# Attention scores in 64-key tiles: five full units for two head groups, an output product in two phases, tokens ahead of weights

## The chip, the core and the metric

The kernel runs on one core of a Trainium2 chip. The metric is the device time of one execution in microseconds; lower is better. On the core, PE (TensorE) multiplies matrices into PSUM, eight banks of 512 fp32 columns on 128 partitions; ACT (ScalarE) evaluates exponentials and GELU; DVE (VectorE) and POOL (GpSimd) do elementwise work; SP issues most DMAs.

## What is computed

Two equal layers over 2048 tokens of width 576. Each is a residual attention block and a residual MLP block:

```python
x = x + _A_ref(_layernorm(x), A_wqkv, A_wo)      # 32 heads of 18, causal, window 256
x = x + _B_ref(_layernorm(x), B_w1, B_b1, B_w2, B_b2)   # 576 -> 4608 -> 576, tanh GELU

scores = jnp.einsum("bhqd,bhkd->bhqk", q, k) * (Dh ** -0.5)
mask = (idx[:, None] - idx[None, :] >= 0) & (idx[:, None] - idx[None, :] < W)   # W = 256
p = _softmax(jnp.where(mask, scores, -1e9))
o = jnp.einsum("bhqk,bhkd->bhqd", p, v)
```

A query sees itself and the 255 tokens before it. Data are bf16; the residual is kept in fp32.

## The kernel before

The work is cut into eight chunks (`CH`, k = 0 to 7): layer 0 has chunks 0 to 3, layer 1 chunks 4 to 7, each of four token tiles of 128. In a chunk, `qkv` projects the normalized tokens, `E` does attention for eight head groups g of four heads j, `tail` multiplies by `wo` and adds the residual, `G_part` does the first MLP product with GELU in three parts, `mm2` the second. Attention of chunk k is interleaved with the MLP of chunk k-1.

Each head's 18 values are padded to 32, so the four heads of a group stand on four 32-row strips of `qT` and `kT`, and four matmuls work side by side in the array. Scores are computed transposed, keys on partitions and queries in columns. `units_of` lists which 128-key tiles meet which queries. A 128-key tile needs three query tiles (its own, partly masked, the next, and the one after, partly masked), so the six key tiles that touch a chunk take 1 + 2 + 3 + 3 + 2 + 1 = 12 blocks of 128 columns, in three units of 512 columns for each group. Chunks 0 and 4 have no earlier keys and take 9 blocks, in units of 384, 512 and 256 columns.

`scores` (L777) issues a unit: its matmuls (L789) go to two pairs of PSUM banks, one bank for a head; two exponentials on ACT (L798), each over two heads, write `pT`; POOL zeroes the masked triangles by `affine_select` (L819). `pT` has PS = 6 slots. `pv` (L824) multiplies all units of a group by the values: 24 matmuls (L834) over 128 key rows, each 20 columns wide (18 values and a column of ones for the softmax's denominator), the four heads on four 32-column strips, into one bank of 7, 6, 5, 4 (`OUT`, shared with `FILL`, the banks of `qkv`, `tail` and `mm2`). DVE transposes the result (L845), takes the reciprocal of the denominator and scales (L851).

The matmuls of `qkv` and `tail` share L699; `G_part` starts each six blocks with six 64-row matmuls (L919) and goes on with 128-row ones (L931); `mm2` is L960.

What decides the order is a planner, `Plan.schedule`. Every operation is a task with an estimated cost, a priority and data dependences; the planner places the task that can start first on its engine, and the order so made is written out with semaphores. `PL.nudge` holds a table of offsets to the priorities by stage, `SWITCH` is the cost charged for a change of PE's tiling (`mode`), and `fifo` keeps tasks of one kind in the order of their listing. Within PE no semaphore is waited for, since matmuls there are in order.

At the start, SP loads the tokens of chunk 0 into `w2_sb` (as `x_in`), ACT issues the six loads of `wqkv` and then loads its table; DVE clears the four output banks (L601), and then layer norm of the four tiles (L620, L643), a transpose on PE (L657) and the projections follow.

Of the kernel before, what the change touches and what calls it, by code (L numbers as in the profile page):

```python
# [40 lines left out]
class Sched:  # L41
# [23 lines left out]
    def add(self, eng, fn, reads=(), writes=(), dma=None, ring=4):  # L65
# [11 lines left out]
        for w in writes:  # L77
            for rd in self.readers.get(w, ()):
                if rd[2] != eng or rd[3]:
                    want(rd[:3])  # L80
            lw = self.last_write.get(w)
            if lw is not None and not (eng == "pe" and lw[2] == "pe"):
                want(lw)
# [76 lines left out]
class Task:  # L160
    __slots__ = ("idx", "eng", "fn", "reads", "writes", "cost", "lat", "prio", "dma", "ring", "handles", "alloc", "move", "desc",
                 "npred", "succ", "ready", "end", "plain", "fifo", "hold", "stage", "mode")
# [24 lines left out]
class Plan:  # L187
# [18 lines left out]
    def add(self, eng, fn, reads=(), writes=(), dma=None, ring=4, cost=0.1, lat=0.1, prio=0.0, alloc=(), fifo=None, plain=False, after=(), move=0.0, desc=0, hold=False, mode="f"):  # L206
# [4 lines left out]
                 plain=plain, move=move, desc=desc, fifo=fifo, hold=hold, stage=stage, mode=mode)  # L211
# [31 lines left out]
    def keep_warm(self, a, b, bank_free, extra):  # L243
# [5 lines left out]
        if n < 1 or not banks:  # L249
# [4 lines left out]
                 dma=None, ring=4, alloc=(), handles=(), plain=False, move=0.0, desc=0, fifo=None, hold=False, stage="", mode="f")  # L254
        extra.append((a, t))

    def schedule(self):
# [56 lines left out]
        while len(order) < n:  # L314
# [80 lines left out]
            for s, data in t.succ:  # L395
                same = s.eng == t.eng == "pe"
                s.ready = max(s.ready, st + t.cost + (t.lat if data and not same else 0.0))
                s.npred -= 1
                if s.npred == 0:
                    released[s.eng].append(s)  # L400
# [3 lines left out]
        for st, t in order:  # L404
# [3 lines left out]
            else:  # L408
                self.S.add(t.eng, t.fn, names(t.reads), names(t.writes), dma=t.dma, ring=t.ring)
# [8 lines left out]
FEED_UNTIL = 40.0  # L418
# [3 lines left out]
def build_kernel(nc, A_x, A_wqkv, A_wo, B_x, B_w1, B_b1, B_w2, B_b2, out):  # L422
# [11 lines left out]
    CUTS = (0, 3, 6, 8)  # L434
# [6 lines left out]
    PS = 6  # L441
    PVG = [()] * 8
    PVLAG = 1
# [6 lines left out]
    NQN = 6  # L450
    WB = 6
    TOPF = D - 512

# [9 lines left out]
    PL.nudge = {"b": 29.4, "ea0": -2.66, "ld0": 0.01, "ld0+": -29.79, "eb0": 0.53, "ec0": 3.31, "le0+": 114.63, "q1.0": -118.82, "q1.1":  # L463
                -98.11, "q1.2": -0.91, "q1.3": -7.44, "t0": -5.22, "ea1": -89.48, "ga0": -171.5, "ga0+": 5.04, "eb1": -15.16, "ma0": 12.04,
                "ma0+": -17.91, "gb0": -145.98, "ec1": -2.99, "le1+": 16.44, "le1": -20.83, "mb0": -3.03, "q2.1": 45.54, "q2.2": 88.61,
                "q2.3": 55.86, "t1": -120.53, "gc0": -19.84, "gc0+": -25.1, "ln3": 57.08, "mc0": 4.28, "mc0+": 148.11, "ga1": -4.06, "ga1+":
                -6.33, "eb2": -3.01, "ma1": 5.64, "ma1+": 13.09, "gb1": -0.44, "ec2": 3.21, "mb1": 7.94, "mb1+": -24.34, "q3.0": 14.13,
                "q3.1": 131.09, "q3.2": 4.89, "q3.3": 1.84, "t2": -15.58, "gc1": 7.36, "gc1+": -31.57, "mc1": 17.31, "mc1+": -1.81, "ga2":
                -27.48, "ga2+": 158.23, "eb3": 36.01, "ma2": 50.85, "ma2+": 24.11, "gb2": 23.88, "gb2+": 71.77, "ec3": -0.31, "mb2": 60.21,
                "mb2+": -145.98, "q4.0": 0.58, "q4.1": 63.81, "q4.2": 55.53, "t3": 61.03, "gc2": 154.1, "gc2+": 8.93, "ln5": 14.44, "ea4":  # L470
                19.04, "mc2": 63.19, "ga3": 18.64, "ga3+": 0.44, "eb4": 14.59, "ma3": 30.2, "ma3+": 0.16, "gb3": -9.23, "gb3+": -6.16,
                "mb3": 45.14, "q5.0": 113.74, "q5.1": 29.89, "q5.2": -8.93, "q5.3": 76.56, "t4": -2.66, "gc3": 88.61, "gc3+": -48.97, "ln6":
                -15.57, "ea5": -72.82, "mc3": -2.47, "mc3+": 76.5, "ga4+": -33.16, "eb5": 2.91, "ma4": 29, "ma4+": 17.98, "gb4": -4.52,
                "gb4+": -7.43, "mb4": 59.81, "mb4+": -8.12, "q6.0": 1.38, "q6.1": 19.98, "q6.2": -18.44, "q6.3": 63.81, "gc4": 92.87,
                "gc4+": 84.52, "ln7": 31.11, "ea6": -2.66, "mc4": 24.73, "mc4+": 0.51, "ga5": 11.4, "ga5+": 1.49, "eb6": -0.34, "ma5":
                52.45, "ma5+": -6.49, "gb5": -32.33, "gb5+": 51.26, "ec6": -3.2, "mb5": 0.24, "mb5+": -3.62, "q7.0": 24.18, "q7.2": 137.8,
                "q7.3": 1.6, "t6": -24.34, "gc5": 5.59, "gc5+": -171.5, "ea7": 41.87, "mc5": 136.49, "mc5+": -1.6, "ga6": -32.64, "eb7":
                31.31, "ma6": 44.85, "ma6+": -1.66, "gb6": 0.02, "gb6+": -4.59, "ec7": -0.12, "mb6": 104.87, "mb6+": 63.38, "t7": -16.91,
                "gc6+": -0.75, "mc6": -119.39, "mc6+": -8.02, "ga7": -61.44, "ga7+": -11.43, "ma7": -14.13, "ma7+": 9.77, "gb7": 1, "mb7":
                3.96, "mb7+": -8.3, "gc7": 53.28, "mc7": 65.68, "": 0.88}  # L480
# [26 lines left out]
    rstd = sb("rstd", [P, NT], FP32)  # L507
    warm = sb("warm", [P, 256], BF16)
    ident = sb("ident", [P, P], BF16)
    b1in = sb("b1in", [NF, P], BF16)  # L510
# [43 lines left out]
    def dma(q, out_, in_, reads=(), writes=(), cls="w", ring=8, **kw):  # L554
# [4 lines left out]
        kw.setdefault("move", n / (330e3 if cls != "xr" else 165e3))  # L559
# [24 lines left out]

    w_load(0)
# [13 lines left out]
    for i in OUT:  # L599
        b = Bank((i,))  # L600
# [545 lines left out]
```

## Time and profile before

| | |
|---|---|
| median of 3 runs | 894.56 us (893.44 to 896.13) |
| profiled execution: its time | 897.23 us |
| its span, first to last instruction | 895.5 us |
| mean granted clock of PE | 0.998 |
| PE busy | 864.4 us (97%) |
| ACT busy | 615.8 us (69%) |
| DVE busy | 410.1 us (46%) |
| POOL busy | 366.2 us (41%) |

The busy time of PE is that of pipelined matmuls, whose recorded lengths overlap: a 288-column matmul is recorded with 286 ns, but the next starts 122.5 ns later. What a burst of matmuls costs is therefore read from its first start to the first start of the burst after it. Groups of instructions are named by the line that issued them, an engine and the tiles written and read; the time behind the last bar is how long the engine was idle before them, with the instruction that ended most of it.

### The profile page before, as it was taken

The page shows a single profiled execution, that of the slowest core. Times are in us where ns is not written, and L with a number is a line of the kernel's source. Part 1 is how long each engine was busy: PE and PEld are TensorE (multiplying, and loading weights), DVE is VectorE, ACT ScalarE, POOL GpSimd, SP SyncE. Part 2 cuts the span into 40 slices and gives each one's busy share as a digit, 9 for nine tenths or more (in the row PEclk, how much of TensorE's full clock was granted, in tenths as well). Part 3 has the DMA queues.
Part 4 walks back from the last instruction along what each step waited for, and adds up shares of the span by engine and source line. Part 5 has one row for each costly group of instructions (what it writes and reads, how often), then busy time and mean ns, then how long its engine had stood idle before and what let it go on. Part 6 is the DMA issues. An engine that isn't in the chain of part 4 may idle for free.

```text
span 895.5 us, 19577 instructions
## 1 busy us (share of the span) xinstructions
PE 864.4 (97%) x7849; PEld 506.5 (57%) x7901; DVE 410.1 (46%) x969; ACT 615.8 (69%) x737; POOL 366.2 (41%) x504
## 2 busy tenths in 40 slices
PE   5898999999999999999999999999999999999998
PEld 4555455656566565665655655556556545556665
DVE  6789223863357351763427633375134523161111
ACT  3976888577767788366773868747777689844443
POOL 3677544274244662224431544416444266231100
PEclk9999999999999999999999999999999999999999
DMA  6788537742477333853457342682537632446431
GB/s 177 139 172 173 179 119 182 178 109 81 149 166 158 120 120 98 183 124 121 130 119 181 71 158 86 143 198 67 165 119 147 184 125 71 144 126 176 153 96 50
DMA packets 182649, 122.25 MB, mean 137 GB/s; under 512 B 107424, under 2 KB 181024, under 8 KB 182560
## 3 DMA queue, kind: packets, MB, share of 16 engines
q1 hardware_dynamic: 179152, 115.47, 49.5%
q0 software_dynamic: 1584, 3.54, 1.5%
q10 hardware_dynamic: 1824, 1.99, 0.7%
q8 instruction: 63, 1.03, 0.5%
q14 instruction: 26, 0.21, 0.1%
HBM read 91.28 MB, written 2.36 MB: 105 GB/s over the span
## 4 chain that ended last, share of the span: by engine, by line
PE 54%; DVE 1%; issue 1%; DMA 1%; ACT 1%; POOL 0%
PE ps L960 21%; PE ps L931 18%; PE ps L699 6%; PE ps L789 3%; PE ps L919 3%; PE ps L834 3%; ACT pT L798 1%; DVE x_res L880 0%; DMA xnTa<-xn 0%; DVE st_all L620 0%; DMA xnTm<-xn 0%; DVE xn L643 0%; DVE xn L648 0%; POOL rstd L633 0%; DVE xn L883 0%
## 5 line engine op out<-in xcount | busy, mean ns | idle before, releaser
L819 POOL TENSOR_SCALAR_AFFINE_SELECT pT<-pT 128x512 bf16<-128x512 bf16 (+1 forms) x368 | 283.5, 794 | 266.6 <-ACT pT L798 262.0
L798 ACT ACTIVATE pT<-ps 128x1024 bf16<-128x1024 f32 (+2 forms) x384 | 345.8, 972 | 58.3 <-PE ps L789 57.8
L934 ACT ACTIVATE hT<-ps,b1col 128x512 bf16<-128x512 f32 x288 | 197.8, 687 | 192.8 <-PE ps L931 188.3
L960 PE MATMUL ps<-w_sb,hT 128*128 128x288 bf16 x2304 | 309.5, 287 | 0.2
L960 PEld LDWEIGHTS ps<-w_sb,hT 128*128 128x128 bf16 x2304 | 213.9, 98 | 81.9 <-issue 24.9
L931 PE MATMUL ps<-xnTm,w_sb 128*128 128x512 bf16 x1100 | 255.0, 380 | 4.9 <-issue 3.2
L931 PEld LDWEIGHTS ps<-xnTm,w_sb 128*128 128x128 bf16 x1152 | 109.6, 98 | 137.0 <-issue 19.1
L880 DVE TENSOR_TENSOR x_res<-ps,x_res 128x288 f32<-128x288 f32 x216 | 95.9, 448 | 169.0 <-PE ps L960 158.4
L699 PE MATMUL ps<-wqkv,xnTa 128*128 128x288 bf16 x960 | 136.0, 289 | 3.5 <-DVE qn L742 1.9
L845 DVE STREAM_TRANSPOSE oq<-ps 128x512 f32<-128x512 f32 x64 | 45.8, 715 | 179.0 <-PE ps L834 178.8
L699 PEld LDWEIGHTS ps<-wqkv,xnTa 128*128 128x128 bf16 x960 | 88.4, 98 | 41.4 <-issue 7.8
L742 DVE CAST qn<-ps 128x288 bf16<-128x288 f32 x120 | 53.2, 449 | 35.1 <-PE ps L699 33.0
L942 POOL TENSOR_TENSOR x_res<-x_res,b2bc 128x576 f32<-128x576 f32 x32 | 40.8, 1274 | 69.2 <-ACT hT L934 69.2
L789 PE MATMUL ps<-qT,kT 32*128 32x384 bf16 (+2 forms) x1216 | 64.1, 276 | 2.2 <-ACT pT L798 2.0
L631 POOL TENSOR_SCALAR vtmp<-mv_all 128x1 f32<-128x1 f32 (+1 forms) x43 | 8.5, 197 | 121.4 <-DVE mv_all L622 120.6
L834 PE MATMUL ps<-pT,vA 128*20 128x384 bf16 (+2 forms) x1408 | 50.7, 276 | 2.0 <-ACT pT L798 0.9
L620 DVE BATCH_NORM_STATS2 st_all<-x_res 128x6 f32<-128x288 f32 x104 | 44.8, 448 | 1.2
L919 PE MATMUL ps<-xnTm,w_sb 64*128 64x512 bf16 x288 | 39.7, 381 | 5.5 <-ACT pT L798 3.3
L789 PEld LDWEIGHTS ps<-qT,kT 32*128 32x128 bf16 x1216 | 19.5, 92 | 44.1 <-issue 25.1
L699 PE MATMUL ps<-wo_sb,attT 128*128 128x288 bf16 x320 | 42.8, 286 | 0.1
L834 PEld LDWEIGHTS ps<-pT,vA 128*20 128x20 bf16 x1408 | 25.7, 90 | 26.8 <-issue 13.4
L729 DVE CAST vA<-ps 128x288 bf16<-128x288 f32 x64 | 28.8, 454 | 23.7 <-PE ps L699 23.4
(47 smaller groups left out, 347.6 us busy)
## 6 DMA issues: line engine op xcount, KB each, us to landing
w_sb<-in_B_w_dram SPq DMA_DIRECT2D x48, 864.0 KB, 5.4
w_sb<-in_B_w_dram SPq DMA_DIRECT2D x48, 768.0 KB, 4.7
w_sb<-in_B_w_dram SPq DMA_DIRECT2D x96, 48.0 KB, 4.4
x_res<-in_A_x_dram POOLq DMA_DIRECT2D x3, 1152.0 KB, 7.0
out_dram<-xn SPq DMA_DIRECT2D x16, 144.0 KB, 1.8
wqkv<-in_A_wqkv_dram ACTq DMA_DIRECT2D x3, 576.0 KB, 6.9
w_sb<-in_A_x_dram SPq DMA_DIRECT2D x2, 576.0 KB, 4.2
wo_sb<-in_A_wo_dram SPq DMA_DIRECT2D x4, 144.0 KB, 2.6
```

The lines of the kernel that those rows point to most:

```text
L699: ins = e.matmul(bank(bs[o])[:, 0:HB], lhs(c), rhs(c, o * HB), start=(c == 0), stop=(c == KD - 1))
L742: add("dve", lambda e, b=bs[o], dst=dst: e.tensor_copy(dst, heads_of(bank(b))), reads=[bs[o]], writes=[f"qn{sl}h{o}"], cost=0.375, lat=0.1 ...
L789: ins = e.matmul(two(bs[j // 2])[:, j % 2, col:col + nq * 128], k_of(T0 + so)[0][32 * j:32 * j + 32, g, :], qs[32 * j:32 * j + 32, g, qo * ...
L798: add("act", lambda e, h2=h2: e.activation(pT[:, sl, 2 * h2:2 * h2 + 2, lo:hi], two(bs[h2])[:, :, lo:hi], ACT.Exp, scale=SCALE), reads=[bs ...
L819: add("pool", lambda e, ap=ap, pat=pat, sgn=sgn, kind=kind: e.affine_select(ap, ap, pattern=pat, compare_op=(ALU.is_ge if kind == "d" else ...
L834: ins = e.matmul(bank(bo)[32 * j:32 * j + VW, qo * 128:(qo + nq) * 128], vA[:, (T0 + so) % VS, 8 * j + g, :], pT[:, sl, j, col:col + nq * ...
L845: add("dve", lambda e: e.transpose(oq[:, 0:4 * nt, :].rearrange("p b c -> p (b c)"), bank(bo)[:, 0:nt * 128]), reads=[bo, f"aq{(g - 1) % G ...
L880: add("dve", lambda e: e.tensor_tensor(x_res[:, t, sl], bank(b)[:, 0:HB], x_old[:, t, sl], ALU.add), reads=[b] + ([f"xin{t}"] if first els ...
L919: ins = e.matmul(bank(bk)[:, 0:n], w1_sb[64 * b:64 * b + 64, sl, col:col + 128], xnTm[64 * b:64 * b + 64, k % 2, 4, 0:n], start=True, stop ...
L931: ins = e.matmul(bank(bk)[:, 0:n], w1_sb[:, sl, col:col + 128], xnTm[:, k % 2, c, 0:n], start=False, stop=(c == 3))
L934: add("act", lambda e, ff=ff, fl=fl, bk=bk: e.activation(hT[:, fl, 0:n], bank(bk)[:, 0:n], ACT.Gelu_apprx_tanh, bias=b1col[:, ff:ff + 1]), ...
L960: ins = e.matmul(bank(b)[:, 0:HB], hT[:, fl, i * 128:(i + 1) * 128], w2_sb[:, fl, hh * HB:(hh + 1) * HB], start=(fl == 0), stop=(fl == NFH ...
```

## The change

Chunks 1 to 7 (`NEW`) compute scores with 64-key tiles: the two halves b of a key tile go to the two 64-column halves of the array, so that a burst uses eight tiles of 32 rows by 64 columns. A 64-key tile needs 320 queries. All blocks of two head groups fill five units of 512 columns exactly in both halves: two for each group alone, and one shared. Chunk 4 takes two units for a group. A unit is 24 or 28 matmuls of 64 to 320 columns (chunk 4: 28 or 16), and its segments are issued by their first column. In the lists of `units_n` a segment is (group, key tile, first query, end, column); `A` and `B` are the two halves.

The output product of two groups (`pv_n`) uses eight tiles of 64 rows by 32 columns. Its two row halves may not write the same bank at once, so phase 0 multiplies half 0 of the first group and half 1 of the second, and phase 1 the others. Phase 1 waits for phase 0 by a semaphore (`own`); the planner may put other work between.

Masks: triangles on half 0, and on both halves, stay selects on POOL; the far triangle on half 1 is a minimum with a constant tile `mk` on DVE. The copy of the last 64 normalized columns for the MLP moves from DVE to POOL. `pT` has 7 slots instead of 6, `qn` 4 instead of 6. At the start, ACT's table load stands before its weight loads, PE clears the output banks by matmuls on a zero tile, and the third token load waits for `q2` instead of `k3`. Several cost estimates, the cuts of `E` and the whole table of nudges differ, so the order of instructions differs everywhere.

```diff
@@ Sched.add, Plan.add: a PE task may wait for an earlier PE task
-            if lw is not None and not (eng == "pe" and lw[2] == "pe"):
+            if lw is not None and (own or not (eng == "pe" and lw[2] == "pe")):
                 want(lw)
@@ build_kernel
-FEED_UNTIL = 40.0
+FEED_UNTIL = 0.0
-    CUTS = (0, 3, 6, 8)
+    CUTS = (0, 4, 6, 8)
-    PS = 6
-    PVG = [()] * 8
-    PVLAG = 1
+    PS = 7
+    LAG = 2
+    NEW = tuple(range(1, 8))
-    NQN = 6
+    NQN = 4
...
+    add("act", lambda e: e.preload_act_table_set("exp_and_others"), cost=1.3, lat=0.0, fifo="act", plain=True, prio=-10)
     w_load(0)
...
-    for i in OUT:
-        b = Bank((i,))
-        add("dve", lambda e, b=b: e.memset(bank(b), 0.0), writes=[b], cost=0.56, lat=0.1, prio=-7, alloc=[b])
+    for i in OUT:
+        b = Bank((i,))
+        def clear(e, b=b):
+            for h in range(2):
+                ins = e.matmul(bank(b)[:, 256 * h:256 * h + 256], warm[:, 0:128], warm[:, :], start=True, stop=True)
+            return ins
+        add("pe", clear, reads=["warm"], writes=[b], cost=0.45, lat=0.2, prio=-7, alloc=[b])
...
-            add("dve", lambda e: e.tensor_scalar(xn[:, sl, D:KD * 128], s[:, t, 512:D], mv_all[:, t, 0:1], rstd[:, t:t + 1],
...
+            add("pool", lambda e: e.tensor_copy(xn[:, sl, D:KD * 128], xn[:, sl, 512:D]), reads=[f"xn{sl}"], writes=[f"xd{sl}"], cost=0.24,
...
+    def units_n(k):
+        A, B = [], []
...
+        A.append([(0, 3, 448, 512, 0), (0, 3, 384, 448, 64), (0, 0, 0, 320, 128), (0, -2, 0, 64, 448)])
+        B.append([(0, -2, 0, 128, 0), (0, 3, 448, 512, 128), (0, 0, 64, 384, 192)])
+        A.append([(0, -1, 0, 192, 0), (0, 1, 128, 192, 192), (0, 2, 256, 512, 256)])
+        B.append([(0, -1, 0, 256, 0), (0, 1, 192, 256, 256), (0, 2, 320, 512, 320)])
+        shared = [([(0, 1, 192, 448, 0), (1, 1, 384, 448, 256), (1, 1, 192, 384, 320)],
+                   [(0, 1, 256, 512, 0), (1, 1, 448, 512, 256), (1, 1, 256, 448, 320)])]
+    def scores_n(k, gs, u, prio):
...
+            segs = sorted([(x[4], b, x) for b in range(2) for x in u[b]])
+            for _, b, (gi, so, lo, hi, col) in segs:
+                for j in range(4):
+                    ins = e.matmul(two(bs[j // 2])[64 * b:64 * b + 64, j % 2, col:col + hi - lo],
+                                   k_of(T0 + so)[0][32 * j:32 * j + 32, gs[gi], 64 * b:64 * b + 64],
+                                   qs[32 * j:32 * j + 32, gs[gi], lo:hi], start=True, stop=True, tile_position=(32 * j, 64 * b))
...
+                add("dve", lambda e, ap=ap, mo=mo: e.tensor_tensor(ap, ap, mo, ALU.min),
...
+    def pv_n(k, gs, segs, prio):
+        bo = [Bank(OUT) for _ in gs]
+        def part(ph, b):
+            return [x for x in segs if x[0] == b and x[1] == (ph if b == 0 else 1 - ph)]
...
+                for j in range(4):
+                    ins = e.matmul(bank(bo[gi])[32 * j:32 * j + VW, lo:hi], vA[64 * b:64 * b + 64, (T0 + so) % VS, 8 * j + gs[gi], :],
+                                   pT[64 * b:64 * b + 64, sl, j, col:col + hi - lo], start=(ph == 0 and gi not in begun),
+                                   stop=(ph == 1 and not any(x[1] == gi for x in seq[n + 1:])), tile_position=(64 * b, 32 * j), skip_group_check=True)
...
+        for ph in range(2):
+            add("pe", lambda e, ph=ph: fn(e, ph), reads=rd, writes=bo, cost=0.045 + ncol * 0.000417, prio=prio - 0.1 * ph, lat=0.25, mode="c",
+                alloc=(bo if ph == 0 else ()), fifo="pv", own=(ph == 1))
...
-    xin_load(8, 4, ["k3"], -4)
+    xin_load(8, 4, [GX], -4)
```

## The prediction

> **What bounds the kernel now.** I read the page first, then the order of the matmuls in the timeline, then who waits for whom, then the two stretches where the tensor engine (PE) is not full.
>
> ```profile
> span 895.5 us, 19577 instructions
> ...
> PE 864.4 (97%) x7849; PEld 506.5 (57%) x7901; DVE 410.1 (46%) x969; ACT 615.8 (69%) x737; POOL 366.2 (41%) x504
> ...
> PE   5898999999999999999999999999999999999998
> ...
> ACT  3976888577767788366773868747777689844443
> ...
> L819 POOL TENSOR_SCALAR_AFFINE_SELECT pT<-pT 128x512 bf16<-128x512 bf16 (+1 forms) x368 | 283.5, 794 | 266.6 <-ACT pT L798 262.0
> L798 ACT ACTIVATE pT<-ps 128x1024 bf16<-128x1024 f32 (+2 forms) x384 | 345.8, 972 | 58.3 <-PE ps L789 57.8
> ...
> L789 PE MATMUL ps<-qT,kT 32*128 32x384 bf16 (+2 forms) x1216 | 64.1, 276 | 2.2 <-ACT pT L798 2.0
> ...
> L834 PE MATMUL ps<-pT,vA 128*20 128x384 bf16 (+2 forms) x1408 | 50.7, 276 | 2.0 <-ACT pT L798 0.9
> ```
>
> PE is busy from slice 3 to the end; ACT has a third of the span free. So a matmul column saved is time saved, and a saved exponential counts only where PE waits for ACT. What attention costs PE is read from start to start in the PE timeline (start, length, line, count):
>
> ```profile
> 295.06 0.65 PE L960 MATMUL ps<-w_sb,hT 128*128 128x288 bf16 x4
> 295.64 0.83 PE L834 MATMUL ps<-pT,vA 128*20 128x384 bf16 x24
> 296.41 0.40 PE L789 MATMUL ps<-qT,kT 32*128 32x384 bf16 x8
> 296.74 1.64 PE L960 MATMUL ps<-w_sb,hT 128*128 128x288 bf16 x12
> 298.31 0.40 PE L789 MATMUL ps<-qT,kT 32*128 32x256 bf16 x8
> 298.64 1.65 PE L960 MATMUL ps<-w_sb,hT 128*128 128x288 bf16 x12
> ```
>
> The trace's own starts sharpen these: an output product holds PE for 766 ns, a 512-column score unit for 330, and the first of them after full-array matmuls comes 95.5 ns late (218 instead of 122.5). 1536 columns at 2.4 GHz are 640 ns, so 126 ns of the 766 are not streaming, and 117 of the unit's 330. About 95 ns of either belongs to the change of tiling, since it is paid once more on the way in. Inside a burst little is lost: the four tiles start 3.4 ns apart, and in the 24 matmuls of 0.83 us the last set (273 ns long) starts 551 ns after the first, where 1280 columns are 533: five successions, two of them behind 128-column sets, lose 18 ns together.
>
> Then the two stretches with holes, the start (timeline) and chunk 7 (PE's waits in 720 to 810 us, and two rows of the table by stretch: length, then PE, PEld, DVE, ACT, POOL busy, clock, DMA):
>
> ```profile
> 2.74 2.11 DVE L601 MEMSET ps<- 128x512 f32 x4
> ...
> 4.75 0.76 DVE L620 BATCH_NORM_STATS2 st_all<-w_sb 128x6 f32<-128x288 bf16 x2
> ...
> 10.72 1.39 PE L699 MATMUL ps<-wqkv,xnTa 128*128 128x288 bf16 x5
> ...
> 21.27 0.78 PE L699 MATMUL ps<-wqkv,xnTa 128*128 128x288 bf16 x5
> ```
>
> ```profile
> PE ps L919 <- ACT pT L798: 3.3, 3, 1.5
> PE ps L919 <- DVE xn L643: 1.0, 1, 1.0
> ```
>
> ```profile
> 80.00:90.00 10.00, 7.39 (x99) 3.87 (x91) 9.84 (x25) 7.75 (x9) 8.16 (x12) 1.00 0.36 70
> ...
> 720.00:730.00 10.00, 7.86 (x94) 4.19 (x88) 4.02 (x9) 9.15 (x10) 7.73 (x11) 0.91 0.57 182
> ```
>
> Five QKV matmuls take 1.39 us at 10.7 us and 0.78 at 21.3: the array runs at half speed until 14.8 us. At 720 us ACT is full (9.15 of 10), PE is not, and the granted clock falls to 0.91.
>
> **Part by part, against the profiled execution (span 895.5, its time 897.23, which is 2.67 above the median 894.56).**
>
> *Score units.* Six chunks lose one unit in six, chunk 4 one in three, chunk 0 none. Before: 160 units of 512 columns (330 ns), 16 of 384 (274) and 16 of 256 (220): 60.7 us. After: 136 units of 512 and chunk 0's 24 old ones. A new unit is 24 or 28 matmuls on eight tiles (32 rows by 64 columns); the trace has no such burst. The floor is today's 330, the ceiling 543 (the halves one after the other, 213 more). I take the floor, plus four more tile starts of 3.4 ns, plus two more successions of 2.5: 348, since rows and columns each run four streams at once here already. 136 x 348 + 8 x (330 + 274 + 220) = 53.9 us.
>
> *Output product.* Before: 48 x 766 + 16 x 602 = 46.4 us. After: per pair of head groups two phases of 1280 columns on eight tiles (64 rows by 32), each 533 + 126 + 14 + 7 = 680 ns, with a ceiling of 1213 if the row halves take turns; chunk 4's eight phases are 1024 columns, 567 ns; chunk 0's eight stay at 602. 48 x 680 + 8 x 567 + 8 x 602 = 42.0 us.
>
> *Tiling changes.* In the built instruction order PE goes from full-array matmuls into scores, product or the 64-row MLP start 246 times before (161, 39, 46) and 228 times after (139, 48, 41), at 95.5 ns: 23.5 and 21.8 us.
>
> *The added wait.* The second phase waits for the first one's results. In 25 of 28 pairs the order puts something between, six full-array matmuls (0.73 us) or a score unit (0.35) mostly, which outlast a 273 ns matmul's drain; queued behind the wait on PE is whatever its order has next, and ACT waits for the score units among it. In 3 pairs nothing stands between: 0.25 each, 0.8 us. Cover gone everywhere would be 7.
>
> PE's sum: 130.6 before, 118.5 after: **-12.1 us**, on the path wherever PE is full.
>
> *Exponentials and masks.* Full 1024-element activations go from 320 to 288, the short ones from 64 to 32: about 29 us less of ACT (1025, 810 and 609 ns each), hidden except at the ends. POOL has 312 selects of 512, 96 of 256 and 8 of 1024 elements a partition instead of 256 and 112: at 650 ns, 1125 and some 410 by their slope, 251 us for 288, off the path. The 32 copies of 64 columns that POOL takes over (nearest row: a 261 ns memset) stand behind selects of up to 1.1 us between layer norm and MLP; PE is full then. DVE gets 136 minima. Nearest rows: 374 ns for 64 elements, 524 for 288, so some 0.5 and 0.67 us, 80 us in all, less the 12 us of those copies. Beside PE that is free (DVE 46% busy), except in 80 to 90 us, where DVE is at 9.84 of 10: about ten of chunk 1's units now precede the first MLP (nine before), with 6 us of minima. I charge 1 us of 0 to 6.
>
> *Start.* The table load goes ahead of ACT's six weight DMAs (1.28 us later for them, which frees the transfer for the tokens), and the four bank memsets (2.11 us, directly ahead of the first statistics) leave DVE for PE: I take 1.5 us, of 0 to 2.1. Eight clearing and 33 warm matmuls fill PE's empty first 9 us, so the projections need not start at half speed: transposes and 30 QKV matmuls run 2.8 us longer than at full rate, of which I take 2.0, the rest going into waits for casts. Together **-3.5**, 0 to -4.9. One cast buffer pair fewer (NQN 4) and the reordered loads of biases and later tokens I cost at nothing: QKV of the next chunk runs a chunk ahead; without that cover the row of casts waiting for a transpose (1.4 us in all) would grow.
>
> *Chunk 7.* PE waits 5.3 us in 720 to 810 and loses about 1.5 to the clock behind them (23 MLP matmuls in 6.32 us from 729.3 on, 5.13 elsewhere). ACT has 8.2 us less of exponentials in this chunk. I take **-4.5** of 0 to -7.
>
> Sum: -12.1 - 3.5 + 1.0 - 4.5 = -19.1, so 878.1 for an execution like the profiled one and **875.4** on the median's scale. With all small terms at their ends: 871 to 888.
>
> **Rivals.**
>
> *The two halves take turns (slower).* Then a unit lasts 543 and a phase 1213: 136 x 0.213 + 48 x 0.533 + 8 x 0.427 = +58 us, giving 933. It decides from a third of that loss on, where the gains are eaten. For it: no row shows row and column tiles mixed. Against: L834's four column tiles stream four different inputs over the same rows at once, 3.4 ns apart. Chance 0.08. In "TensorE: Matmul & The Clock Gate" (Part 3) the Trainium skill reports sixteen row-and-column tiles at 10.6 times one; no run here shows that.
>
> *A short matmul must wait for a longer one issued before it.* In the trace all four tiles always carry equal lengths, so ends in program order cost nothing. Now lengths differ: in the first unit the order is 64, 128, 64, 320, 64, 320, 64 columns on alternating halves, and if the third 64 may end only after the 320 ahead of it, its half idles. Working the lists through with 2.4 columns a ns, the units last 125 and 98 ns more (the shared one none), the phases 68 and 144: 0.66 us a pair, 0.4 in chunk 4, +17.4 in all, giving 893, no change to be measured. Chance 0.09. This is the Trainium skill's rule in the same Part 3, that matmuls both start and end in program order; the trace agrees as far as it goes, since its sets start and end in order.
>
> *Short segments don't hide the next weights.* A tile's next weights load while its present matmul runs. 128 columns (53 ns) suffice here; 64 (27 ns) are nowhere seen. If a 64-column segment lasts 53 ns, units last 79, 53 and 26 ns more and phases 120 to 132: +14.3, giving 890. Chance 0.13. "TensorEngine Tiling (Array Packing)", Instruction Overhead, in the Trainium skill puts some 60 cycles on every matmul and advises against cutting a dimension that is already small; as an estimate from it, 25 ns a segment would cost 23 us, giving 898. The 3.6 ns a succession above speak against it.
>
> *PSUM.* A pair now holds two of the four output banks through both phases. PE's waits for DVE to free a bank are 2.9 us now; trebled they give 881. This stays in the forecast's range.
>
> **How the numbers follow.** Forecast 0.65, rivals 0.08, 0.09 and 0.13, the rest (0.05) more waits than I see. A difference under 0.3% (2.7 us) can't be told from none. Faster: the forecast, the third rival and a part of the second, 0.86; same 0.06; slower 0.08. The range, 862 to 892, reaches from a start and chunk 7 without holes, with waits elsewhere shrinking too, to just short of the second rival.
>
> **What would show it.** A new unit at 0.35 us from start to start (0.40, 0.47 or 0.56 by the rivals); a phase at 0.68 (0.80, 0.75 to 0.82, or 1.21); PE busy near 852; five QKV matmuls in 0.78 us from the first on, that first one at 9 to 9.5 us; PE's waits for ACT in chunk 7 under 2 us. A phase over 0.9 would make the prediction wrong, and so would DVE at 10 of 10 with PE idle before the first MLP.

## The result: slower by 0.4%

| | before | changed |
|---|---|---|
| median | 894.56 us | 897.85 us |
| runs | 893.44 to 896.31 | 895.90 to 900.57 |
| ratio, with its 95% interval | 1 | 1.0037 (1.0019 to 1.0054) |
| profiled execution, its span | 895.5 us | 895.6 us |

The forecast was 875.4 us. The change did most of what it said it would do to the tensor engine, and the time did not follow. The page of the changed kernel, and behind it the line of the instruction queue in the kernel before:

```profile
span 895.6 us, 28477 instructions
...
PE 867.0 (97%) x12247; PEld 533.7 (60%) x12247; DVE 478.1 (53%) x1071; ACT 567.8 (63%) x673; POOL 355.0 (40%) x583
...
PE   8898899989999999999999999999999989999998
...
q8 instruction: 96, 1.57, 0.7%
```

```profile
q8 instruction: 63, 1.03, 0.5%
```

PE is busy 867.0 us where 852 was forecast; the empty first slices are filled with warm matmuls, and 8s now stand among the 9s. ACT is down by 48 us, DVE up by 68. The last line counts packets of instructions, 96 of them against 63 in the kernel before. That they are PE's own is read from the numbers: both counts keep step with PE's matmuls and weight loads, about 250 to a packet.

What attention costs PE, from start to start in the PE timeline:

```profile
294.82 1.63 PE L735 MATMUL ps<-wqkv,xnTa 128*128 128x288 bf16 x12
296.39 0.43 PE L921 MATMUL ps<-qT,kT 32*64 32x64 bf16 x28
296.75 0.79 PE L735 MATMUL ps<-wqkv,xnTa 128*128 128x288 bf16 x5
297.46 0.79 PE L1006 MATMUL ps<-pT,vA 64*20 64x128 bf16 x64
298.19 0.79 PE L735 MATMUL ps<-wqkv,xnTa 128*128 128x288 bf16 x5
298.91 0.79 PE L1006 MATMUL ps<-pT,vA 64*20 64x128 bf16 x64
```

L921 is a new unit, 0.36 us; L1006 a phase, 0.72. Over the whole trace a unit takes 361 ns (348 forecast), a phase 724 (680), a phase of chunk 4 586 (567), a change of tiling 95 as before. Scores, products and changes together fall from 130.4 to 121.5 us: 8.9 us won, where 12.1 were forecast with 0.8 for an added wait in them. What PE spends otherwise without streaming (the span less all bursts from start to start) rises from 38.4 to 47.4 us and eats exactly that. So the question is what PE waits for. First the list of the kernel before, then that of the changed one, from the top, the latter with all lines that name "issue":

```profile
PE ps L657 <- DVE xn L643: 9.1, 1, 9.1
PE ps L919 <- ACT pT L798: 3.3, 3, 1.5
PE ps L931 <- issue: 3.2, 19, 0.3
PE ps L789 <- ACT pT L798: 2.7, 8, 0.7
PE ps L699 <- DVE qn L742: 1.9, 5, 0.7
```

```profile
PE ps L735 <- DVE qn L783: 2.7, 5, 1.5
PE ps L693 <- DVE xn L680: 1.9, 3, 1.2
PE ps L1114 <- DVE xn L1074: 1.8, 1, 1.8
PE ps L735 <- DVE x_res L1071: 1.8, 3, 1.2
PE ps L735 <- DVE oq L1023: 1.7, 1, 1.7
PE ps L921 <- DVE oq L1023: 1.5, 1, 1.5
PE ps L1114 <- issue: 1.3, 1, 1.3
PE ps L735 <- issue: 1.3, 2, 0.9
...
PE ps L1006 <- issue: 1.0, 1, 1.0
...
PE ps L1114 <- ACT pT L817: 0.4, 2, 0.2
```

Two things are new. The waits for ACT, 6.9 us in the list of before, are 1.3. Their place is taken by DVE: leaving out the wait for the first tokens (9.1 us before; 1.9 and 1.1 for warm data now), its lines sum to 5.1 us before and 13.5 now. And 3.6 us are put down to "issue": PE waited for nothing that the profile shows. (The 3.2 us of "issue" in the kernel before are 19 gaps of at most 0.3 us, each the room of one matmul whose record is missing.) A third thing is no wait: the planner fills holes that it foresees in PE's first 140 us with matmuls on a zero tile. Behind the first 20 us the changed kernel has 25 of them and the kernel before 8, some 1.9 us more (17 at 0.11); whether PE would have stood idle there without them is not shown.

DVE's groups, by shape, give the first a cause:

```profile
L963 DVE TENSOR_TENSOR pT<-pT,mk 64x512 bf16<-64x512 bf16 x72 | 38.1, 528 | 20.2 <-ACT pT L817 17.7
L1029 DVE TENSOR_TENSOR attq<-oq,rinv 128x288 bf16<-128x288 f32 x64 | 36.5, 570 | 1.2
L963 DVE TENSOR_TENSOR pT<-pT,mk 64x256 bf16<-64x256 bf16 x64 | 36.2, 565 | 12.0 <-ACT pT L817 10.3
```

The short minimum, half the elements, lasts longer than the long one. Single ones last up to 1662 ns; a long one that met no POOL instruction took 422. POOL's selects of 128x512 take 666 ns alone and 778 with a minimum beside them. That the two engines hold each other up is what the experiments test.

The second shows itself in the PE timeline, where a step of six matmuls without any semaphore inside stops after the fourth:

```profile
153.59 0.79 PE L1006 MATMUL ps<-pT,vA 64*20 64x128 bf16 x64
154.34 0.61 PE L1114 MATMUL ps<-xnTm,w_sb 64*128 64x512 bf16 x4
156.26 0.39 PE L1114 MATMUL ps<-xnTm,w_sb 64*128 64x512 bf16 x2 [1.31 <-issue]
```

In the trace's packet records an instruction packet of 16,384 bytes started at 153.44 us and had landed at 154.95; PE went on 1.31 us later. 24,494 matmuls and weight loads and 282 instructions of PE's sequencer, over 96 packets, are 258 to a packet; 256 of 64 bytes each would fill one. The four stops of this kind, at matmuls 2115, 2621, 4269 and 9590, stand 1,024, 3,328 and 10,751 instructions apart when the sequencer's are counted, that is 4.00, 13.00 and 42.00 packets, and each ends 1.0 to 1.4 us after a packet has landed.

### The profile page after: what moved, and what is told of

Same layout as the page of the kernel before. It is cut to its first block, busy times and chain, and to the rows that moved or that the text cites. A ratio compares the mean times of both kernels' runs of the same rounds, so it can differ in the third digit from the quotient of the medians.

```text
span 895.6 us, 28477 instructions
## 1 busy us (share of the span) xinstructions
PE 867.0 (97%) x12247; PEld 533.7 (60%) x12247; DVE 478.1 (53%) x1071; ACT 567.8 (63%) x673; POOL 355.0 (40%) x583
## 4 chain that ended last, share of the span: by engine, by line
PE 85%; DVE 5%; POOL 3%; issue 3%; ACT 2%; DMA 2%; SPq 0%; ACTq 0%; DVEq 0%; POOLq 0%
PE ps L1157 30%; PE ps L1126 28%; PE ps L735 13%; PE ps L1006 5%; PE ps L921 4%; PE ps L1114 4%; ACT pT L817 2%; POOL pT L866 2%; DVE pT L963 1%; POOL pT L974 1%; DMA w_sb<-in_B_w_dram 1%; DVE st_all L657 1%; DVE x_res L1071 1%; DMA xnTa<-xn 1%; DMA w_sb<-in_A_x_dram 0%
## 5 line engine op out<-in xcount | busy, mean ns | idle before, releaser
L817 ACT ACTIVATE pT<-ps 128x1024 bf16<-128x1024 f32 (+1 forms) x320 | 297.4, 990 | 87.3 <-PE ps L921 76.6
L974 POOL TENSOR_SCALAR_AFFINE_SELECT pT<-pT 64x512 bf16<-64x512 bf16 (+2 forms) x376 | 235.0, 653 | 256.6 <-ACT pT L817 255.7
L1126 PE MATMUL ps<-xnTm,w_sb 128*128 128x512 bf16 x1152 | 260.5, 379 | 0.0
L963 DVE TENSOR_TENSOR pT<-pT,mk 64x512 bf16<-64x512 bf16 (+1 forms) x136 | 74.2, 546 | 32.2 <-ACT pT L817 27.9
L921 PE MATMUL ps<-qT,kT 32*64 32x64 bf16 (+4 forms) x2912 | 49.7, 238 | 1.2 <-DVE x_res L1071 0.8
L1006 PE MATMUL ps<-pT,vA 64*20 64x64 bf16 (+4 forms) x3424 | 43.6, 231 | 3.0 <-issue 1.0
L735 PE MATMUL ps<-wo_sb,attT 128*128 128x288 bf16 x320 | 44.9, 286 | 0.6 <-DVE x_res L1071 0.3
L921 PEld LDWEIGHTS ps<-qT,kT 32*64 32x64 bf16 x2912 | 27.4, 103 | 28.7 <-issue 15.1
L1006 PEld LDWEIGHTS ps<-pT,vA 64*20 64x20 bf16 x3424 | 33.1, 84 | 19.1 <-issue 9.2
```

The costliest lines, as they stand in the source:

```text
L735: ins = e.matmul(bank(bs[o])[:, 0:HB], lhs(c), rhs(c, o * HB), start=(c == 0), stop=(c == KD - 1))
L817: add("act", lambda e, h2=h2: e.activation(pT[:, sl, 2 * h2:2 * h2 + 2, 0:ncol], two(bs[h2])[:, :, 0:ncol], ACT.Exp, scale=SCALE), reads=[ ...
L921: ins = e.matmul(two(bs[j // 2])[64 * b:64 * b + 64, j % 2, col:col + hi - lo], k_of(T0 + so)[0][32 * j:32 * j + 32, gs[gi], 64 * b:64 * b ...
L963: add("dve", lambda e, ap=ap, mo=mo: e.tensor_tensor(ap, ap, mo, ALU.min), reads=[f"p{sl}h0", f"p{sl}h1", "mask"], writes=[f"p{sl}m{mi}"], ...
L974: add("pool", lambda e, ap=ap, pat=pat, sgn=sgn, b=b: e.affine_select(ap, ap, pattern=pat, compare_op=(ALU.is_ge if sgn == 1 else ALU.is_g ...
L1006: ins = e.matmul(bank(bo[gi])[32 * j:32 * j + VW, lo:hi], vA[64 * b:64 * b + 64, (T0 + so) % VS, 8 * j + gs[gi], :], pT[64 * b:64 * b + 64 ...
```

## The experiments

Three theories were set against each other. **A**: minima and selects hold each other up, DVE is late with casts and with freeing PSUM banks, and PE, whose order is fixed, waits. **B**: the new start and chunk 0 cost it. **D**: the short matmuls use up instruction packets faster than they come. (C, in the first expectations, is that the planned order was fitted to times that the chip does not keep.) "Order unchanged" means that every engine has the same instructions in the same order. Differences between kernels are differences of their ratios to the kernel before, times 895 us; with the intervals of both ratios such a difference is good to about 2 us.

**Minima cut (e1).**

```diff
+                ap, mo = pT[64:128, sl, 0, c:c + 1], mk[64:128, 0:1]
                 add("dve", lambda e, ap=ap, mo=mo: e.tensor_tensor(ap, ap, mo, ALU.min),
```

> The 136 minima on VectorE are cut to one column each (64x1 instead of 64x256 or 64x512); everything else, and the order of every engine, stays as in the changed kernel. Left out: the far triangle's mask on the lower 64 keys. Theory A (minima on VectorE and selects on GpSimd hold each other up, VectorE is late in freeing PSUM banks and TensorE waits for it): the minima's 136 x about 0.5 us go, their stretching of the selects goes, TensorE's idle time falls by 5 to 9 us, 889 to 893 us. Theory B (the new start and chunk 0's later scores cost it, in the first 100 us): 897 to 898, as before that edit. Theory C (many small shortfalls against the planned times, spread over all engines): 895 to 897.

Measured: 892.06 us, ratio 0.9962 (0.9945 to 0.9978), 6.7 us under the changed kernel. As A has it. "Issue" stays, at 5.0 us: the same four stops at the same matmuls, and a fifth at 972.

**Selects cut (e2).**

```diff
+            ap, pat = pT[0:(128 if b else 64), sl, :, c:c + 1], [[0, 4], [sgn, 1]]
             add("pool", lambda e, ap=ap, pat=pat, sgn=sgn, b=b: e.affine_select(
```

> GpSimd's selects of chunks 1 to 7 are cut to one column per head (the near triangle's masks and the upper 64 keys' far masks are left out); the minima on VectorE and the order of every engine stay. Theory A: the selects no longer stretch minima, quotients and normalizations, VectorE is on time; 888 to 892 us, the rows of the minima near their lone 422 ns. Theory B: 897 to 898. Theory C: 894 to 897, a gain only by what the selects were late for the output product (ScalarE's and GpSimd's waits of TensorE).

Measured: 891.25 us, 0.9958 (0.9939 to 0.9978), 7.1 us under. DVE's groups by shape in this kernel:

```profile
L963 DVE TENSOR_TENSOR pT<-pT,mk 64x512 bf16<-64x512 bf16 x72 | 30.5, 424 | 25.0 <-ACT pT L817 22.6
L963 DVE TENSOR_TENSOR pT<-pT,mk 64x256 bf16<-64x256 bf16 x64 | 18.8, 294 | 13.5 <-ACT pT L817 11.5
```

The same minima in the same places take 49 us instead of 74, and PE's waits for DVE, the first tokens included, fall from 16.5 to 7.6 us. Cutting either partner gives the same 7 us, as it would if it is one loss, the meeting of the two; no run cuts both. The stops stand at the same five matmuls as in e1, and "issue" is 6.7 us, so part of what DVE no longer costs is lost again to the packets.

**Work kept, meeting taken away (e12).** Whether DVE's added work or the hold-up matters is told apart by an operation as long that is not held up; statistics of one input last 448 to 454 ns with and without POOL beside them.

```diff
-                add("dve", lambda e, ap=ap, mo=mo: e.tensor_tensor(ap, ap, mo, ALU.min),
+                w, r = (140 if n == 1 else 264), len([m for m in marks[:mi] if m[:2] == ("o", 1)])
+                add("dve", lambda e, w=w, r=r: e.bn_stats(scr[64:128, sl, r, :], nhalf[64:128, 0:1].to_broadcast([64, w])),
```

> Each minimum on VectorE is replaced by statistics over a constant (64x264 for the long ones, 64x140 for the short), which last about what a minimum lasts alone (422 and 290 ns) and do not stretch against GpSimd (statistics rows of the changed kernel: 454 ns alone, 448 beside GpSimd). Order, selects and all else as in the changed kernel; the far triangle on the lower 64 keys stays unmasked. If the loss is the mutual hold-up of minima and selects: 4 to 7 us under the changed kernel, 891 to 894, like e1_min_1col. If VectorE's 49 us of plain work for the minima is what makes it late: 0 to 2 us under it, 896 to 898.

Measured: 892.91 us, 0.9975 (0.9964 to 0.9987), 5.5 us under. The rows of the replacements:

```profile
L964 DVE BATCH_NORM_STATS2 scr<-nhalf 64x6 f32<-64x264 f32 x72 | 31.1, 432 | 23.4 <-ACT pT L817 21.0
L964 DVE BATCH_NORM_STATS2 scr<-nhalf 64x6 f32<-64x140 f32 x64 | 19.4, 303 | 12.3 <-ACT pT L817 10.4
```

They ran 432 and 303 ns, and the 128x512 selects fell from 758 to 671 ns. So of the 6.7 to 7.1 us, some 5.5 are the hold-up; the 1.2 to 1.6 left for DVE's plain work can't be told from nothing. The replacement reads another tile as well, so e12 alone does not part a shared tile from a shared port. The quotient row does (L1029, `attq<-oq,rinv`): it touches no `pT` and still lasts 454 ns alone and 719 beside POOL. The Trainium skill states such a hold-up in "SBUF — State Buffer", Who interferes with whom: a VectorE operation with both inputs in SBUF contends with a GpSimd operation that reads SBUF, since its second input comes through the read interface that the two share. These rows agree. Two inputs are not the only case in these traces: the normalization (L680, one tile and two scalars a partition) lasts 575 ns alone and 707 beside POOL, and 577 beside it where the selects are cut (e2).

**Instructions moved by 66, 132 and 198 places (e5, e6, e13).** The first warm matmuls, in PE's empty first 9 us, are cut into two, three or four; columns and order unchanged.

```diff
+        cut = 3 if not begun0 else 1
+        begun0.append(n)
-        for _ in range(n):
-            ins = e.matmul(bank(bk)[:, 0:256], warm[:, 0:128], warm[:, :], start=True, stop=True)
+        for _ in range(n * cut):
+            ins = e.matmul(bank(bk)[:, 0:256 // cut], warm[:, 0:128], warm[:, 0:256 // cut], start=True, stop=True)
```

> As the changed kernel, but the first 33 warm matmuls of 256 columns are cut into 66 of 128: 66 more instructions for TensorE in its empty first 9 us, so that all later instructions stand 66 places further on. The order, the work and the plan stay. Theory D (TensorE's instructions come in packets of 16 KB, 256 instructions, and where a packet's worth of short matmuls runs out within some 2.5 us, TensorE stands idle until the next one is there): the gaps at matmuls 2115, 2621, 4269 and 9590 (0.5 to 1.5 us, together 4.2) leave these places; others appear 60 to 130 matmuls away or none do; the time is anywhere from 893 to 899. Theory A (VectorE and GpSimd alone): the gaps stay at the same places in the order, time within 1 us of the changed kernel's.

> The same with the 33 matmuls cut into 99 of 85 columns: all later instructions stand 132 places further on, half a packet. Theory D: gaps at other matmuls again than in the changed kernel and in the shift by 66; 893 to 899. Theory A: as the changed kernel.

> The changed kernel with the first 33 warm matmuls cut into 132 of 64 columns: instructions stand 198 places further on. Idle time put down to issue anywhere between 2 and 10 us (3.6 in the changed kernel, 4.2 shifted by 66, 12.7 by 132), and the time as much above or below 894 as that: 895 to 906.

| shift | median, us | ratio | "issue" in gaps over 0.3 us | span, us |
|---|---|---|---|---|
| 0 (changed) | 897.85 | 1.0037 (1.0019 to 1.0054) | 3.6 | 895.6 |
| 66 | 900.15 | 1.0049 (1.0031 to 1.0066) | 5.2 | 900.5 |
| 132 | 909.58 | 1.0148 (1.0131 to 1.0165) | 12.7 | 905.1 |
| 198 | 894.98 | 1.0004 (0.9991 to 1.0018) | 1.7 | 891.7 |

The four kernels do the same work in the same order. The gaps left the old places each time, and the time follows the column "issue". The shifts by 66 and 132 went past the 899 us that was expected of them, the shift by 198 stayed just under its range. (The 4.2 us that two of the expectations give for "issue" are 3.6 in the changed kernel and 5.2 in the shift by 66.) PE's waits and timeline in the shift by 132:

```profile
PE ps L1009 <- issue: 8.1, 6, 2.3
```

```profile
343.43 0.66 PE L1009 MATMUL ps<-pT,vA 64*20 64x128 bf16 x50
346.41 0.36 PE L1009 MATMUL ps<-pT,vA 64*20 64x192 bf16 x14 [2.33 <-issue]
```

A phase of 64 matmuls stands still after 50. The shift by 66 is not told by packets alone: its span is 4.9 us longer with 1.6 us more of "issue", and its trace shows two windows at half clock (6.8 us at 90.6, 3.4 at 735.7), which the changed kernel's has not. That execution is also the slowest of six.

**The control: the same shift in the old scheme (e8, e14).** e8 is the kernel before with two parts of the new start alone:

```diff
+    add("act", lambda e: e.preload_act_table_set("exp_and_others"), cost=1.3, lat=0.0, fifo="act", plain=True, prio=-10)
     w_load(0)
...
-        add("dve", lambda e, b=b: e.memset(bank(b), 0.0), writes=[b], cost=0.56, lat=0.1, prio=-7, alloc=[b])
+        add("pe", clear, reads=["warm"], writes=[b], cost=0.45, lat=0.2, prio=-7, alloc=[b])
```

> The kernel before with two parts of the change alone: ScalarE's table load ahead of its weight loads, and the four output banks cleared by eight matmuls instead of four memsets on VectorE. Everything else, the table of priorities too, as before; planned 1.4 us earlier. The prediction's start (a gain of 3.5 us, 0 to 4.9): 891 to 893. Theory B (the new start costs): 895 to 898.

> The control: the old scheme with the new start (e8_old_new_start) and the same shift by 132 places that cost the changed kernel 10 us. If it is the new scheme's dense bursts of short matmuls that run into the instruction packets: within 1.5 us of e8_old_new_start, 895 to 898, no idle time put down to issue beyond the 0.2 us gaps of missing records. If any change of the start's matmuls moves the time: 900 or more.

Measured: e8 896.61 us, 1.0014 (1.0004 to 1.0024); e14 894.16, 0.9989 (0.9979 to 0.9999). In e8 the first QKV matmul comes 0.6 us earlier than before and the first scores 0.9, but the first MLP 1.0 us later (93.5 us against 92.5). The windows of before, of e8 and of e14:

```profile
20.00:60.00 40.00, 36.14 (x415) 20.90 (x412) 33.42 (x83) 34.79 (x49) 26.48 (x37) 1.00 0.79 155
```

```profile
20.00:60.00 40.00, 33.21 (x384) 18.92 (x385) 31.07 (x78) 33.13 (x47) 25.77 (x37) 1.00 0.75 150
```

```profile
20.00:60.00 40.00, 36.04 (x412) 20.55 (x413) 32.39 (x79) 35.39 (x51) 27.94 (x40) 1.00 0.82 154
```

In e8's trace PE gives back before 60 us what it gained before 20 (busy 33.21 instead of 36.14). But that execution is the slowest of ten, 3.3 us above their median, and 1.5 us of it is one wait for a DMA (`qT<-qn`) that e14's trace has not. e14, with the same start, keeps the gain: 36.04 busy, the first MLP at 90.5 us, and a median 1.0 us under the kernel before. So the two parts of the start are worth between -1.0 and +1.3 us, not the 3.5 of the prediction, and a cost of 1.3 is too small for theory B to be the whole answer. The other parts of the start (the third token load, the cuts, the feeding rule) and chunk 0's order under the new table were not tried by themselves.

e14 is the control for D: the shift that costs the new scheme 10 us costs the old one nothing, and neither has a gap of "issue" above the room of a missing record. It is 2.2 us under e8, more than the 1.5 expected. So a shift can move the time by some 2 us without packets; the shifts of the new scheme by 66 and 198 are of that size (+1.1 and -3.0), and only the one by 132 stands far above it.

**Longer segments (e7), and both losses taken away (e9).**

```diff
-            for _, b, (gi, so, lo, hi, col) in segs:
+            q0 = 128 * min(x[2] // 128 for x in u[0] + u[1])
+            for b, lo, hi, col in [(b, *r) for r in ((q0, 512, 0), (q0, 2 * q0, 512 - q0)) for b in range(2)]:
...
+                    w = min(512, at[b] - c0)
```

> As the changed kernel with the same order, masks and columns streamed, but each half of a score unit is one matmul of 512 columns a head (two where the last queries are not in yet) instead of 3 or 4 segments, and an output phase has segments of up to 512 columns; the products are of wrong tiles, so it is for its time alone. Theory D: no gap that ends 1.0 to 1.7 us after an instruction packet, 4 us less waiting; and units back to 330 to 340 ns, phases to 650 to 690 (another 5 to 7 us): 885 to 889. Theory A: units and phases shorter, VectorE and GpSimd as late as before, TensorE waits for them with what it saves: 892 to 896.

> The long segments of e7_long_segments and the one-column selects of e2_sel_1col together, order unchanged; products of wrong tiles and without the selects' masks. If the collisions on VectorE and GpSimd (7.1 us against the changed kernel) and the instruction packets with the longer instruction stream (8.5 us, of which 4.2 are PE's own shorter units and phases) are two separate losses, they add: 15 us under the changed kernel, 881 to 885 us. If one wait only hides the other: 887 to 890.

Measured: e7 890.55 us, 0.9942 (0.9928 to 0.9957), 8.5 us under the changed kernel, with 7,975 matmul records instead of 12,247 and no "issue" beyond missing records. A unit takes 354 ns, a phase 661, which is 4.2 us less in all; the other 4.3 are about what the packets took. e9 881.09 us, 0.9840 (0.9817 to 0.9862), 17.6 us under: the two losses add (8.5 and 7.1, and 2 more, which the intervals allow). What its PE still waits for, from the top:

```profile
PE ps L735 <- DMA xnTa<-xn: 2.1, 2, 1.5
PE ps L735 <- DVE qn L783: 1.9, 3, 1.5
PE ps L735 <- DVE oq L1034: 1.6, 1, 1.6
```

**Without the table of priorities (e3, e4).** Both have the new start and an empty table; e4 has the old units in all chunks.

```diff
-    PL.nudge = {"b": -0.09, "ln1": -4.49,
+    PL.nudge = {} and {"b": -0.09, "ln1": -4.49,
-    NEW = tuple(range(1, 8))
+    NEW = ()
```

> The changed kernel with an empty table of priorities, so that the planner's order comes from its plain priorities alone; the planned end is 13.4 us later than with the table. Theory A: the loss against the plan comes from operations that get in each other's way wherever they stand, 908 to 914 us. Theory B: as the start's order changes with the table, anything from 900 to 912. Theory C (the table was fitted to planned times which the chip does not keep, so it buys less than planned): 902 to 908, within 10 us of the tuned one.

> As the untuned kernel above, but with 128-key score units and one output product for each group in all chunks (the list of chunks with the new scheme is empty), the start and everything else as in the changed kernel. Planned 15.0 us later than the untuned new scheme; TensorE's own instructions take 8.9 us more (this is what the two traces showed). Theory A: the scheme gives only 0 to 6 us, since it brings the minima and their collisions, so 0 to 6 us above the untuned new one. Theory B: the scheme itself is sound and gives 9 to 15 us. Theory C: 5 to 12 us.

Measured: e3 913.38 us, 1.0195 (1.0176 to 1.0214); e4 910.37, 1.0158 (1.0136 to 1.0179). None of the theories had the new scheme 3 us slower than the old one here. "Issue" is 8.6 us in e3 and none in e4: by size, packets alone take back what the scheme saves on PE. The loss does not hang on the one order that the changed kernel happens to have.

**Other orders (e10, e11).** e10 has another table, found by replaying the order with the durations measured above and a fixed time for each packet; e11 has a third table, searched in the same way, and keeps the two phases of a product apart.

```diff
-            add("pe", lambda e, ph=ph: fn(e, ph), reads=rd, writes=bo, cost=0.045 + ncol * 0.000417, prio=prio - 0.1 * ph, lat=0.25, mode="c",
+            add("pe", lambda e, ph=ph: fn(e, ph), reads=rd, writes=bo, cost=0.045 + ncol * 0.000417, prio=prio - 0.1 * ph, lat=1.2 if ph == 0 else 0.25, mode="c",
```

> The changed kernel with another table of priorities, and nothing else. The table was searched against a replay of the order in which units, phases, minima, selects and quotients last as long as the trace of the changed kernel shows and an instruction packet arrives 3.9 us after the one before it was begun, averaged over alignments. The replay puts it 2.7 us under the changed kernel (from 890.6 to 888.0, the chip's 897.85 for the former). If packets and collisions are what was lost: 893 to 896, no worse than the kernel before. If the cause lies elsewhere: 897 or more.

> The two phases of an output product (128 matmuls, one packet of instructions in 1.45 us) are kept at least 1.2 us apart by the planner, so that long matmuls stand between them; table of priorities searched anew under the same replay. By the packets: idle time put down to issue under 2 us (3.6 in the changed kernel), 894 to 898 us in all, since the replay gives it back 1.5 us to other waits. If packets are not the cause, idle time put down to issue stays at 3 us or more.

Measured: e10 903.73 us, 1.0088 (1.0073 to 1.0103); e11 906.89, 1.0125 (1.0102 to 1.0149). Both missed. In e10 "issue" is 6.3 us and PE's waits for ACT are back at 4.2. By the words of its expectation e10 speaks for another cause; its trace shows packets and late DVE still there (12.2 us of waits), so it tells of the replay more than of the cause. In e11 "issue" fell to 1.9 as expected, but the waits for DMA are 5.7 us (1.8 in the changed kernel), those for DVE hardly less (15.5 against 16.5), there are 15 more changes of tiling, and two windows run at half clock, 3.4 us each. The replay had the mean stretch of an operation and not which two meet, nor when a packet is slow; it was no guide to a better order. Of the versions that leave nothing out, the new scheme's best is the shift by 198, level with the kernel before (1.0004), and the fastest of all is e14 in the old scheme, 0.1% under it.

## Why the prediction was wrong

*Score units, output product.* The mechanism was right, two terms were too small. The halves run independently: 64-column matmuls on one half start 25 to 31 ns apart while a 320-column one runs on the other, so "the two halves take turns" and "a short matmul must wait for a longer one" are out; for the latter, the Trainium skill's rule that matmuls end in program order ("TensorE: Matmul & The Clock Gate", Part 3) would have made a unit of one group 0.45 us or more, and the trace shows 0.36. The added wait, priced at 0.8 us, is about 0.4: each of the three pairs of phases back to back lasts 1.59 us, 0.14 more than two phases. The unit was taken at the floor plus 18 ns and is 31 above it (136 x 13 ns = 1.8 us), the phase at 680 and is 724 (48 x 44 ns = 2.1). e7 says what the phase's excess is: the many short segments, 63 ns a phase. That is a small part of the third rival's +14.3 us; the rest of it did not show in units and phases, and the short segments cost otherwise, by the number of instructions. The rival PSUM had PE's waits for DVE to free a bank trebled, and all its waits for DVE rose from 5.1 to 13.5 us; but e2 and e12 take most of the rise away with the output banks held as before (7.6 and 8.9 us with the first tokens, 16.5 in the changed kernel), so the held banks are not its cause.

*"Beside PE that is free (DVE 46% busy)"* is the step that failed most. It priced minima by rows of operations alone and let only 80 to 90 us suffer, for 1 us. Alone they were cheaper than I thought (290 and 422 ns instead of 500 and 670), but they meet POOL's selects, and both grow (e2, e12). The mean load of DVE said nothing on that; what counts, by PE's list of waits, is when a cast or a freed bank comes in an order that is fixed. It cost some 5.5 us of hold-up (e12) and up to 1.6 of work. *"POOL ... off the path"* fails with it. The kernel before had the sign in its trace: its quotient rows (L851, two SBUF inputs) ran 454 ns alone and 581 beside POOL. Before the first MLP burst, which comes at 97.0 us instead of 92.5, the sign that the prediction named against itself showed in part (before, then changed):

```profile
90.00:100.00 10.00, 9.38 (x54) 4.50 (x56) 2.50 (x6) 7.24 (x10) 5.60 (x6) 1.00 0.55 139
```

```profile
90.00:100.00 10.00, 7.23 (x92) 4.25 (x93) 8.57 (x16) 7.48 (x9) 7.90 (x16) 1.00 0.38 51
```

*Start: -3.5.* One observation came true (the first five QKV matmuls in 0.78 us), one did not (the first of them at 10.22 us, where 9 to 9.5 was named and 10.72 stood before), and the value did not: +1.3 us by e8, -1.0 by e14. The step took a shift at the start for a shift of the end. That ACT, DVE and POOL lead PE's first 90 us, so that it was lost there, is argued and not shown.

*Chunk 7: -4.5.* The waits for ACT before MLP bursts went from 3.3 to 0.4 us and the clock stays full, as forecast; but it stays full there in e8 and e14 as well, whose chunk 7 is the old one, so that this is not shown to be the change's doing. Of the 5.3 us of waits that the term started from, 0.7 were the room of missing records. And in 720 to 730 us other engines are now full (the two windows of the prediction, in the changed kernel):

```profile
80.00:90.00 10.00, 8.12 (x269) 5.24 (x267) 9.69 (x26) 7.73 (x9) 7.97 (x16) 1.00 0.32 80
720.00:730.00 10.00, 8.29 (x292) 5.44 (x291) 7.56 (x13) 9.74 (x11) 9.71 (x18) 1.00 0.19 50
```

POOL, 7.73 of 10 before, is at 9.71 and ACT at 9.74; PE gains 0.43 us of busy time. What PE does not stream in 700 to 800 us falls by 2.0 us. In the first line DVE, at 9.69 of 10, is no fuller than before (9.84), and PE is at 8.12 instead of 7.39.

*Not in the sum at all:* instruction packets, 3.6 us in this kernel's alignment. No view of the kernel before showed a wait of that kind. That a unit would have 24 or 28 matmuls in place of 8 was seen, and priced at 18 ns a unit.

Together, measured against forecast: PE's bursts with the added wait -8.5 (-12.1); start -1.0 to +1.3 (-3.5); minima beside POOL +5.5 to +7.1 (+1.0); chunk 7 -2.0 (-4.5); packets +3.6 (nothing). The measured terms come to -2.4 to +1.5 us, and the spans differ by +0.1; they come from different runs, so the tally is a rough one. The medians differ by 3.3 because the profiled execution before was 2.67 us above its median, the changed one 0.4 under. With hold-up and packets taken away e9 stands at 881.1; the 5.7 us to the forecast are of the size of what start (2.5 to 4.8) and chunk 7 (2.5) fell short, which no run shows by itself.

## What to carry to other kernels

Price an added operation by the operation that will run beside it, and not by the mean load of its engine. Count instructions as well as columns: a scheme that cuts matmuls into short pieces can be right in every duration and still run out of instructions, by an amount that hangs on where the packet boundaries fall; shifting the stream by a few idle instructions is the cheapest test for it. And a saving in one stretch need not arrive at the end: ask which engine leads that stretch.

## What the runs showed of the hardware

- PE's instructions come in packets of 16 KB (256 instructions). A packet took 0.88 to 2.1 us to move, and at most stops PE resumed 1.0 to 1.7 us after it had landed. Call the 256 instructions of a packet a block. In the changed kernel the packet for the next block was begun 0.9 us (at the median) after PE's first matmul of a block, 0.9 to 1.5 us at the four stops. So, as an estimate from these times, a block that runs out in less than about 3.2 us (0.9 + 1.0 + 1.3) can make PE wait. Five of the changed kernel's blocks lasted under 3 us. Four of them ended in its four stops; the packet behind the fifth had been begun 2.0 us before PE reached that block. A pair of phases is 128 matmuls, 256 instructions with their weight loads, in 1.45 us: one packet. In the old units (e4) and in e7 the shortest block lasted about 9 us.
- The Trainium skill, in "Runtime: NRT & Kernel Launch", Instruction fetch mechanics, has the same blocks of 256 instructions and calls the cost of crossing one mostly hidden. The blocks agree with the packets here; that they are hidden holds for the old scheme and not for the new one (1.7 to 12.7 us).
- All eight idle gaps of PE of 1.95 us and more behind the start (1.95 to 3.31), over all runs here, were met by half clock, for 3.4 us or (once) 6.8, so that a long wait is paid again. After gaps of 1.5 to 1.9 us it came at times (1.52 in the kernel before) and at times not (1.74 and 1.79 in the changed one, 1.87 in the shift by 132). In the shift by 132, after the gap of 2.33 us (length, then PE, PEld, DVE, ACT and POOL busy, clock, DMA):

```profile
347.00:350.00 3.00, 2.98 (x7) 1.06 (x7) 2.79 (x7) 0.69 (x1) 0.00 (x0) 0.50 0.00 0
```

- A one-column minimum (64x1, e1) lasted 158 ns the one time that it met no POOL instruction, 249 at the mean and up to 1402: it is held up however little it has to do itself.
